# A fused spectral mixer and GEGLU block on one core: weight forms over five plain chunks, stores three steps later, transposes ahead of the down stage

## The chip, the cores and the metric

The kernel runs on one core of a Trainium2 chip. A core has a matrix engine (PE, with its weight loads PEld beside it), a vector engine (DVE), a scalar or activation engine (ACT), a general engine (POOL) and a queue engine (SP) that issues all of this kernel's DMA transfers. Each engine works through its own instructions in the order of the program and waits on semaphores for the others. The metric is the device time of one execution, the median over several runs.

## The reference

Two blocks act one after the other on 8192 tokens of 448 channels: a spectral block (Fourier transform over the tokens, a small complex two-layer network on each frequency in four channel blocks, soft threshold, inverse transform), and a gated feed-forward block of width 1792. Both are modulated by six rows that come from a condition vector.

```python
x = A_x
mod = (_silu(c) @ w_mod).reshape(c.shape[0], 6, 1, -1)
sa, ca, ga, sb, cb, gb = (mod[:, 0], ..., mod[:, 5])
h = _layernorm(x, axis=-1) * (1 + ca) + sa
x = x + ga * _A_ref(h, A_w1, A_b1, A_w2, A_b2)       # rfft, complex MLP, shrink, irfft
h = _layernorm(x, axis=-1) * (1 + cb) + sb
x = x + gb * _B_ref(h, B_w_gate, B_w_up, B_w_down)   # (gelu(h @ w_gate) * (h @ w_up)) @ w_down
```

## The kernel before

Up to 384.7 us the kernel makes the spectral part: it leaves the half-inverted spectrum in DRAM (`vd`). All that the change touches comes after that.

The second part goes over the tokens in 32 chunks of 256 (`CB` = 2 blocks of 128). For a chunk it loads `v` (spectrum), `g` (a slice of the inverse transform) and `xx` (the input), finishes the inverse transform on PE, adds the residual into a tile `x1`, normalizes to `n`, packs `n` as a high and a low half in float16 into `pk`, and turns `pk` into `nt` by transposing DMA transfers. Then PE forms gate and up products for 1792 columns, ACT and DVE make the activation `x`, it is quantized into two halves `ac`, and the down stage multiplies by `wd` and adds the result to `x1`, which goes to `out`.

There are two ways to form gate and up:

- **Plain chunks**, the first `NSTD` = 4. A chunk has 14 steps k (`gate_up(i, k)`), each 20 products of 128x256. At step k = 2 stands the down stage of the chunk before (`down(i - 1)`), with three places inside it (`mid(0)`, `mid(1)`, `mid(2)`, called m0, m1 and m2 below) where other work may be put.
- **Winograd chunks**, all later ones. They use the Strassen-Winograd scheme: sums and differences of weight parts and of token parts, in 7 products in place of 8. A chunk has 7 periods (`period(u)`), one for each pair of weight tiles, and the down stage of the chunk before stands at period `LA` = 2, in `phase(i)`.

The Winograd scheme needs the weights in another form. In the plain chunks 1 to 3 the kernel makes these forms for 7 weight tiles: `load_forms` loads a tile into `wr`; `form_sums` forms sums on POOL; `forms_hi` writes the high halves into `ws` on ACT (L1557); `forms_lo` writes the low halves on DVE (L1561); `store_forms` sends `ws` to DRAM (`wk`). Each tile has two parts that are stored apart, made of four pieces (0 and 1, 2 and 3). All tiles use one `wr`, and both parts use one `ws`. A table `prep` says after which step each of these calls stands: a tile takes six steps.

In the Winograd chunks PE reads the forms from four slots (`wslot`), which `load_part` refills from `wk` (L1269). `load_part` also fills the slots for the first time, at steps 4, 7, 11 and 13 of the last plain chunk.

Nothing but the order of the program sets which work comes first on an engine: the schedule is written out by hand, in the tables `prep`, `hooks`, `second` and `first` for plain chunks and `extra` for Winograd chunks. In `extra`, a key is the period within the chunk, and each entry names how many chunks ahead it works. The packing (`wpack_hi` on ACT, L1321, and `wpack_lo` on POOL) is held back to the next period. `wtransposes` (L1333) issues the transposes of `pk`, one at period 1 and four at period 2. `phase(i)` comes ahead of the entries of `extra` at period 2, and the store of the output (L1241) is the last thing that `down` issues. The pools `cq`, `cp2` and `wp` hold one buffer for each tag unless a number is given.

The names in the profile: `pgu` and `set` are the PSUM banks of plain and Winograd products, `pdn` those of the down stage, `pi` those of the inverse, `sb` a copy of part of `set` that ACT makes (L1378) and DVE adds back (L1387).

Of the kernel before, what the change touches and what calls it, by code (L numbers as in the profile page):

```python
# [39 lines left out]
LA = 2  # L40
NSTD = 4
WPARTS = ((0, 4), (4, 7))
# [7 lines left out]
def spectral_geglu(ctx, tc, x, w1, b1, w2, b2, wg, wu, wd, cvec, wmod, cf1, cs2, cmi, cgm, out):  # L50
# [924 lines left out]
    with ExitStack() as cctx:  # L975
# [4 lines left out]
        pkt = cp.tile([128, NXT * 128], F16, name="pk")  # L980
        nts, acts, pgu = {}, {}, {}

# [213 lines left out]
        def down(i, banks, mid=lambda n: None):  # L1196
# [43 lines left out]
            if not last:  # L1240
                dma(ov[:, i * CB : (i + 1) * CB, :], x1)  # L1241

# [224 lines left out]
        def phase(i):  # L1467
# [66 lines left out]
        def form_cuts(t, part):  # L1534

            w, r, s2 = raws[("s", t)], raws[("w", t)], raws[("f", t)].rearrange("p (c x) -> p c x", c=3)
            tq = r[:, :, 6:7]
# [25 lines left out]
        def store_forms(t, part):  # L1563
            w = raws.pop(("s", t))
            if part == 0:
                G.tensor_copy(w[:, :, 3, 0:3], w[:, :, 2, 0:3])
            for pr, rows in enumerate(rows2):
                for r, c in zip(rows2, range(2)):
                    dma(wk[t][part][r, pr], w[rows, :, c::2])

        prep = {}
        for n in range(NP):
            for s, fn, *args in (
                (0, load_forms),
                (1, form_sums, 0),
                (1, forms_hi, 0),
                (2, forms_lo, 0),
                (2, forms_hi, 1),
                (2, forms_lo, 1),
                (3, form_sums, 1),  # L1580
                (3, store_forms, 0),
                (4, forms_hi, 2),
                (4, forms_hi, 3),
                (4, forms_lo, 2),
                (5, forms_lo, 3),
                (5, store_forms, 1),
            ):
                prep.setdefault(NFT + 6 * n + s, []).append((fn, n, *args))
        for s, k in enumerate((4, 7, 11, 13)):
            for part in range(2):  # L1590
                prep.setdefault((NSTD - 1) * NFT + k, []).append((lambda u, part: load_part(u, part), U0 + s, part))

# [72 lines left out]
        V.tensor_scalar(gb_r, gb_r, ds_d, None, op0=ALU.mult)  # L1665

        def two_banks(q):
            return bank("pc" if q == 1 else "pd", "pdn")

        def steps0(n):  # L1670
            for fn, *args in second[("down", None, "down2")[n]] if n != 1 else []:
                fn(2, *args)

        for i in range(NSTD):
# [4 lines left out]
            for k in range(NFT):  # L1679
# [5 lines left out]
                if i == 1:  # L1685
                    for fn, *args in second.get(k, []):
                        fn(2, *args)
                if k == 2 and i > 0:
# [21 lines left out]

        load_v(NSTD + 2)
        load_g(NSTD + 2)
        for u in range(U0, NT_ + 1):
            period(u)
            i, k = divmod(u, NP)
            if i == nch:
                continue
            flush()
            if k == LA:
                phase(i)  # L1720
            for d, fn, *args in extra[k]:
                if i + d < nch:
                    if fn in (wpack_hi, wpack_lo):
                        held.append((fn, i + d, *args))
                    else:
                        fn(i + d, *args)
        late = {
            0: lambda: [on(NT_ - 1, joins), on(NT_ - 1, gel3), on(NT_ - 3, quant_lo), on(NT_ - 1, mult3), on(NT_ - 1, stage_d), on(NT_ - 1, gel1), on(NT_ - 1, mult1), on(NT_ - 2, quant_hi), sums(xs[NT_ - 1], V)],
# [79 lines left out]
```

## Time and profile before

| | us |
|---|---|
| Median of 3 runs (lowest to highest) | 2153.84 (2153.24 to 2154.56) |
| Profiled execution, its own time | 2148.29 |
| Span of its instructions | 2146.5 |
| Busy: PE | 1919.0 (89%) |
| Busy: DVE, POOL, ACT | 1467.5, 1177.7, 1022.5 |

A row of a wait list names the waiting engine and line, the one it waited for, the total, the number of times and the longest. A row of a line group names line, engine, operation, out<-in and count, then busy time and the mean of one in ns, then the engine's idle time just before these instructions and what ended most of it. A row of the timeline gives start, length, engine, line and operation, and in brackets the idle time before and its releaser; SPq is the queue of DMA issues. The granted PE clock is a share of full speed, averaged over a stretch.

### The profile page before, as it was taken

The numbers are of one execution on the slowest core, as the hardware profiler recorded it, in microseconds if no ns is written. First come the engines' busy times: TensorE is split into PE (matmuls) and PEld (weight loads), VectorE is DVE, ScalarE is ACT, GpSimd is POOL, SyncE is SP. The second block draws the span as 40 slices with busy tenths as digits, with TensorE's granted clock in tenths as the row PEclk, the third lists the DMA queues.
The fourth block names the chain that finished last, engine by engine and source line by source line (L and its number), as shares of the span: only waits on it lengthen the run. The fifth ranks groups of instructions, "written<-read, shape, count | busy, mean of one in ns | idle before, by whom it ended". The sixth has DMA issues, their size and how long they took to land.

```text
span 2146.5 us, 58651 instructions
## 1 busy us (share of the span) xinstructions
PE 1919.0 (89%) x24284; PEld 1817.2 (85%) x24284; DVE 1467.5 (68%) x2957; ACT 1022.5 (48%) x1915; POOL 1177.7 (55%) x1643
## 2 busy tenths in 40 slices
PE   7899999886673899999999999999989999999998
PEld 3699998775552899999999999999989999999998
DVE  8677887755534576767676677777667676777744
ACT  5687887533322344444444444444444444444443
POOL 3166643455553565656565555666556565655633
PEclk9999999997876899999999999999999999999999
DMA  9998776544455755556565555555555555555562
GB/s 349 317 276 238 179 195 170 154 107 101 97 129 138 213 148 148 153 155 167 149 174 151 163 149 148 148 148 157 153 154 157 164 167 153 148 148 149 147 164 67
DMA packets 410308, 353.83 MB, mean 165 GB/s; under 512 B 115892, under 2 KB 388408, under 8 KB 410040
## 3 DMA queue, kind: packets, MB, share of 16 engines
q1 hardware_dynamic: 410040, 350.08, 57.9%
q8 instruction: 190, 3.11, 0.6%
q14 instruction: 78, 0.64, 0.1%
HBM read 265.34 MB, written 60.10 MB: 152 GB/s over the span
## 4 chain that ended last, share of the span: by engine, by line
PE 52%; DVE 14%; DMA 11%; POOL 9%; SPq 5%; ACT 4%; issue 4%; ACTq 0%; POOLq 0%; DVEq 0%
PE set L1350 25%; PE pdn L1193 4%; DMA nt<-pk 4%; PE pdn L1191 4%; PE pdn L1192 4%; DVE ac L1425 3%; POOL x L1206 3%; POOL o L1205 3%; PE set L1191 2%; PE set L1192 2%; PE set L1193 2%; SPq L1333 2%; DVE ws L1561 1%; DVE y L471 1%; PE ps L210 1%
## 5 line engine op out<-in xcount | busy, mean ns | idle before, releaser
L1350 PE MATMUL set<-nt,wk 128*128 128x128 f16 x15288 | 911.1, 224 | 111.4 <-ACT sb L1378 76.8
L1350 PEld LDWEIGHTS <-wk 128*128 128x128 f16 x15288 | 901.1, 101 | 119.2 <-issue 117.1
L1191 PE MATMUL pdn<-wd,ac 128*128 128x224 f16 x1162 | 303.1, 261 | 12.3 <-ACT ac L1178 11.7
L1193 PE MATMUL pdn<-wd,ac 128*128 128x224 f16 x1162 | 302.7, 260 | 3.3 <-DVE ac L1179 2.1
L1192 PE MATMUL pdn<-wd,ac 128*128 128x224 f16 x1162 | 302.8, 261 | 0.0
L1425 DVE SCALAR_TENSOR_TENSOR ac<-x,sa_act,ac 128x896 f16<-128x896 f32 x196 | 277.0, 1414 | 1.3 <-ACT ac L1415 1.3
L1167 POOL TENSOR_TENSOR x<-x 128x128 f32<-128x128 f32 x223 | 120.3, 539 | 251.4 <-DVE x L1403 142.4
L1403 DVE TENSOR_TENSOR x<-c,gl 128x384 f32<-128x384 f32 x196 | 179.0, 913 | 109.8 <-ACT gl L1399 109.7
L1399 ACT ACTIVATE gl<-c,dg 128x384 f32<-128x384 f32 x196 | 120.5, 615 | 275.1 <-DVE c L1393 271.8
L1415 ACT ACTIVATE ac<-x,sa_act 128x896 f16<-128x896 f32 x196 | 202.3, 1032 | 0.6 <-DVE x L1170 0.4
L1118 PE MATMUL pgu<-nt,wk 128*128 128x256 f16 (+1 forms) x1232 | 154.5, 295 | 44.0 <-DVE x L1159 43.9
L1234 POOL TENSOR_TENSOR o<-u,p 128x224 f32<-128x224 f32 x32 | 21.0, 658 | 306.0 <-DVE u L1233 299.6
L1118 PEld LDWEIGHTS <-wk 128*128 128x128 f16 (+1 forms) x1232 | 121.8, 105 | 76.6 <-issue 54.7
L1387 DVE TENSOR_TENSOR c<-set,sb 128x512 f32<-128x512 f32 x196 | 134.6, 687 | 74.2 <-PE set L1350 74.2
L1191 PEld LDWEIGHTS <-ac 128*128 128x128 f16 x1568 | 154.0, 98 | 19.2 <-ACT ac L1178 12.2
L1193 PEld LDWEIGHTS <-ac 128*128 128x128 f16 x1568 | 154.1, 98 | 4.9 <-DVE ac L1179 2.8
L1192 PEld LDWEIGHTS <-ac 128*128 128x128 f16 x1568 | 154.2, 98 | 0.5
L1378 ACT COPY sb<-set 128x512 f32<-128x512 f32 x196 | 113.7, 580 | 73.1 <-PE set L1350 71.8
L1168 POOL TENSOR_TENSOR x<-x 128x128 f32<-128x128 f32 x223 | 126.6, 568 | 17.5
L471 DVE SCALAR_TENSOR_TENSOR y<-pm,t 64x224 f32<-64x224 f32 x256 | 99.5, 388 | 39.1 <-ACT t L463 35.1
L1327 POOL TENSOR_TENSOR pk<-tf,pk 128x128 f16<-128x128 f32 (+2 forms) x84 | 92.5, 1115 | 52.8 <-ACT pk L1321 52.8
L115 POOL TENSOR_TENSOR yl<-y,yh 128x448 fp32r<-128x448 f32 x63 | 76.6, 1216 | 73.7 <-ACT yh L113 57.9
(323 smaller groups left out, 3970.3 us busy)
## 6 DMA issues: line engine op xcount, KB each, us to landing
wk<-wk SPq DMA_DIRECT2D x88, 1024.0 KB, 7.3
wk<-wk SPq DMA_DIRECT2D x88, 768.0 KB, 5.4
tr<-td SPq DMA_DIRECT2D x64, 224.0 KB, 4.9
vd<-us SPq DMA_DIRECT2D x64, 224.0 KB, 3.1
xx<-in_A_x SPq DMA_DIRECT2D x32, 448.0 KB
v<-vd SPq DMA_DIRECT2D x63, 224.0 KB, 5.5
out<-x SPq DMA_DIRECT2D x31, 448.0 KB
xt<-in_A_x SPq DMA_DIRECT2D x15, 896.0 KB, 16.2
```

What stands on the lines that cost most here:

```text
L471: V.scalar_tensor_tensor(y[ri * 64 : ri * 64 + 64, gi], pv[si, ri], LAM, tv[si, ri], op0=ALU.add, op1=ALU.min)
L1118: T.matmul(pgu[i, t, q][:, pr * H : (pr + 1) * H], ws[rows, n, w, tw], nts[i][rows, tn, :], start=start, stop=stop, skip_group_check=True,)
L1168: e.tensor_tensor(s2, s1, a11, ALU.subtract)
L1191: T.matmul(ps, ac[:, 0, ka], w[:, 0, kb], start=n == 0, stop=False)
L1192: T.matmul(ps, ac[:, 0, ka], w[:, 1, kb], start=False, stop=False)
L1193: T.matmul(ps, ac[:, 1, ka], w[:, 0, kb], start=False, stop=n == NP - 1)
L1350: T.matmul(ps2[:, pr, reg * 128 : reg * 128 + 128], slot[:, pr, hl, wt, :], nt[:, xt, :], start=start and j == 0, stop=j == len(terms) - 1 ...
L1387: V.tensor_tensor(c[:, :, 1:3, :], p[:, :, 0:256].rearrange("p g (r c) -> p g r c", r=2), b[:, :, 0:128].rearrange("p g (o c) -> p g o c", ...
L1399: S.activation(gls[u], cts[u][:, 0], AF.Gelu_apprx_tanh, scale=dg)
L1403: V.tensor_tensor(xs[u][:, 1::3, :], cts.pop(u)[:, 1], gls.pop(u), ALU.mult)
L1415: S.activation(ac[:, 0], xs[u][:, 0:7], AF.Copy, scale=sa_act[:, t : t + 1])
L1425: V.scalar_tensor_tensor(ac[:, 1], xs.pop(u)[:, 0:7], sa_act[:, t : t + 1], ac[:, 0], op0=ALU.mult, op1=ALU.subtract)
```

## The change

`NSTD` becomes 6, so 6 chunks are plain and 26 take the Winograd way. The forms are made in chunks 1 to 5. Their calls are placed by a time in us within the plain stage (33 us from tile to tile), which `plan` turns into a step or one of the places m0 to m2 of the down stage by a list of 48.2 us for a chunk. Part 0 and part 1 each have a `ws` of their own. Calls of `prep` now stand ahead of the down stage at step 2. The output's store is taken out of `down`: `store_out` issues it after the down stage of step 5 in plain chunks and after period 4 in Winograd chunks (`down` stands at 2 in both). In `extra` the split of `v` moves to period 0, the loads of `v` and `g` for the next chunks change places, and `phase` comes after the entries of period 2. The token sums of chunks 6 and 7 use the buffer `o` of the down stage. `v` and `g` of chunk 8 are loaded at step 9 of the last plain chunk; before, those of chunk 6 were loaded after it.

```diff
-NSTD = 4
+NSTD = 6
@@ down
             if not last:
-                dma(ov[:, i * CB : (i + 1) * CB, :], x1)
+                outs.append((i, x1))
@@ token_sums
-                nxt[i]["t"] = cq.tile([128, 2 * D], F32, tag="tf", name="tf")
+                nxt[i]["t"] = cq.tile([128, 2 * D], F32, tag="o", name="tf") if i < NSTD + 2 else cp2.tile([128, 2 * D], F32, tag="tf", name="tf")
@@ extra
-            0: [],
-            1: [(2, split_v), (2, split_g), (1, wtransposes, [0])],
+            0: [(2, split_v)],
+            1: [(2, split_g), (1, wtransposes, [0])],
...
-            5: [(2, wpack_hi, [3]), (2, wpack_lo, [3]), (3, load_g)],
-            6: [(2, wpack_hi, [4]), (2, wpack_lo, [4]), (3, load_v)],
+            5: [(2, wpack_hi, [3]), (2, wpack_lo, [3]), (3, load_v)],
+            6: [(2, wpack_hi, [4]), (2, wpack_lo, [4]), (3, load_g)],
@@ forms_hi
-                raws[("s", t)] = cp2.tile([128, 2, 4, 4 - part // 2, 128], F16, tag="ws", name="ws")
+                raws[("s", t, part // 2)] = cp2.tile([128, 2, 4, 4 - part // 2, 128], F16, tag=f"ws{part}", name="ws")
@@ the table of the forms
+        spots = [(0, 2.4), (1, 4.9), (2, 7.3), ("m0", 11.3), ("m1", 13.3), ("m2", 17.4)]
+        spots += [(k, 21.4 + 2.44 * (k - 2)) for k in range(3, NFT)]
         prep = {}
+        def plan(us, fn, *args):
+            i, r = divmod(us, 48.2)
+            i, p = next(((1 + int(i), p) for p, at in spots if at >= r), (2 + int(i), 0))
+            prep.setdefault((i, p), []).append((fn, *args))
         for n in range(NP):
-            for s, fn, *args in (
+            for us, fn, *args in (
                 (0, load_forms),
-                (1, form_sums, 0),
-                (1, forms_hi, 0),
...
-                (5, store_forms, 1),
+                (11, form_sums, 0),
+                (11, forms_hi, 0),
...
+                (28, store_forms, 1),
             ):
-                prep.setdefault(NFT + 6 * n + s, []).append((fn, n, *args))
+                plan(33 * n + us, fn, n, *args)
@@ the plain chunks
+                for fn, *args in prep.pop((i, k), []):
+                    fn(*args)
                 if k == 2 and i > 0:
-                    down(i - 1, two_banks, steps0 if i == 1 else lambda n: None)
+                    down(i - 1, two_banks, lambda n: steps_std(i, n))
...
+                if k == 5:
+                    store_out()
+                if (i, k) == (NSTD - 1, 9):
+                    load_v(NSTD + 2)
+                    load_g(NSTD + 2)
-                for fn, *args in first.pop(i * NFT + k, []) + prep.pop(i * NFT + k, []):
+                for fn, *args in first.pop(i * NFT + k, []):
@@ the Winograd chunks
             if i == nch:
                 continue
+            if k == LA + 2:
+                store_out()
             flush()
-            if k == LA:
-                phase(i)
             for d, fn, *args in extra[k]:
...
+            if k == LA:
+                phase(i)
```

Two places show what this does to the order of the engines. The first is SP's queue in an early Winograd chunk, chunk 5 of before and chunk 7 of the change: `wk<-wk` is a refill of a slot, `nt<-pk` the transposes, `out<-x` the store, and `v`, `g` and `xx` the loads. Before:

```order
L1333 DMA_TRANSPOSE nt<-pk 128x5x128
L1269 DMA wk_3379<-wk_65 128x8x384
L1269 DMA wk_3377<-wk_60 128x8x512
L1241 DMA out<-x_5746 128x896
L1333 DMA_TRANSPOSE nt<-pk 128x5x128 x4
L1269 DMA wk_3378<-wk_63 128x8x384
L1269 DMA wk_3377<-wk_61 128x8x384
L909 DMA g<-cgm 128x256
L911 DMA xx<-in_A_x 128x896
L917 DMA v<-vd 128x2x224 x2
```

With the change:

```order
L1333 DMA_TRANSPOSE nt<-pk 128x5x128
L1269 DMA wk_3379<-wk_65 128x8x384
L1269 DMA wk_3377<-wk_60 128x8x512
L1333 DMA_TRANSPOSE nt<-pk 128x5x128 x4
L1269 DMA wk_3378<-wk_63 128x8x384
L1677 DMA out<-x_3369 128x896
L1269 DMA wk_3377<-wk_61 128x8x384
L917 DMA v<-vd 128x2x224 x2
L909 DMA g<-cgm 128x256
L911 DMA xx<-in_A_x 128x896
```

The four transposes have moved ahead of the store, the store stands behind one more refill, and `v` comes ahead of `g`.

The second place is ACT in plain chunk 1, from the end of the first weight tile's forms (`ws<-wr`) to the start of the second's; `gel` is the activation of a gate and up step and `ac` the quantization. Before:

```order
L1557 ACTIVATE ws<-wr,sww 128x256
L1154 ACTIVATE gel<-pgu,dg 128x256
L1178 ACTIVATE ac<-x_6737,sa_act 128x896
L1154 ACTIVATE gel<-pgu,dg 128x256 x2
L1178 ACTIVATE ac<-x_6785,sa_act 128x896
L1557 ACTIVATE ws<-wr,sww 128x3x128
L1557 ACTIVATE ws<-wr,sww 128x128
```

With the change:

```order
L1557 ACTIVATE ws<-wr,sww 128x256
L113 CAST gh<-g 128x256
L113 CAST vh<-v 128x896
L1154 ACTIVATE gel<-pgu,dg 128x256 x2
L1178 ACTIVATE ac<-x_6738,sa_act 128x896
L1154 ACTIVATE gel<-pgu,dg 128x256 x2
L1178 ACTIVATE ac<-x_6795,sa_act 128x896
L1154 ACTIVATE gel<-pgu,dg 128x256 x2
L1178 ACTIVATE ac<-x_6894,sa_act 128x896
L1154 ACTIVATE gel<-pgu,dg 128x256 x2
L1178 ACTIVATE ac<-x_6937,sa_act 128x896
L1154 ACTIVATE gel<-pgu,dg 128x256
```

Between two tiles' forms stood three activations, and now there are nine; the next row of the change is the second tile's first form.

More of the change, by code (lines that the diff above doesn't have):

```diff
@@ L980, in spectral_geglu @@
         pkt = cp.tile([128, NXT * 128], F16, name="pk")
-        nts, acts, pgu = {}, {}, {}
+        nts, acts, pgu, outs = {}, {}, {}, []
         def nt_tile():
@@ L1534, in form_cuts @@
         def form_cuts(t, part):
-            w, r, s2 = raws[("s", t)], raws[("w", t)], raws[("f", t)].rearrange("p (c x) -> p c x", c=3)
+            w, r, s2 = raws[("s", t, part // 2)], raws[("w", t)], raws[("f", t)].rearrange("p (c x) -> p c x", c=3)
             tq = r[:, :, 6:7]
@@ L1563, in store_forms @@
         def store_forms(t, part):
-            w = raws.pop(("s", t))
+            w = raws.pop(("s", t, part))
             if part == 0:
@@ L1569, in store_forms @@
                     dma(wk[t][part][r, pr], w[rows, :, c::2])
+        spots = [(0, 2.4), (1, 4.9), (2, 7.3), ("m0", 11.3), ("m1", 13.3), ("m2", 17.4)]
+        spots += [(k, 21.4 + 2.44 * (k - 2)) for k in range(3, NFT)]
         prep = {}
+        def plan(us, fn, *args):
+            i, r = divmod(us, 48.2)
+            i, p = next(((1 + int(i), p) for p, at in spots if at >= r), (2 + int(i), 0))
+            prep.setdefault((i, p), []).append((fn, *args))
         for n in range(NP):
-            for s, fn, *args in (
+            for us, fn, *args in (
                 (0, load_forms),
-                (1, form_sums, 0),
-                (1, forms_hi, 0),
[L1577 to L1585, printed above, removed]
-                (5, store_forms, 1),
-            ):
-                prep.setdefault(NFT + 6 * n + s, []).append((fn, n, *args))
-        for s, k in enumerate((4, 7, 11, 13)):
+                (11, form_sums, 0),
+                (11, forms_hi, 0),
+                (11, forms_lo, 0),
+                (14, forms_hi, 1),
+                (14, forms_lo, 1),
+                (17, form_sums, 1),
+                (19, store_forms, 0),
+                (20, forms_hi, 2),
+                (20, forms_lo, 2),
+                (23, forms_hi, 3),
+                (23, forms_lo, 3),
+                (28, store_forms, 1),
+            ):
+                plan(33 * n + us, fn, n, *args)
+        for n, k in enumerate((4, 7, 11, 13)):
             for part in range(2):
-                prep.setdefault((NSTD - 1) * NFT + k, []).append((lambda u, part: load_part(u, part), U0 + s, part))
+                prep.setdefault((NSTD - 1, k), []).append((lambda u, part: load_part(u, part), U0 + n, part))
         hooks = {
@@ L1665, in spectral_geglu, with store_out, steps_std @@
         V.tensor_scalar(gb_r, gb_r, ds_d, None, op0=ALU.mult)
+        def store_out():
+            for i, x1 in outs:
+                dma(ov[:, i * CB : (i + 1) * CB, :], x1)
+            outs.clear()
         def two_banks(q):
             return bank("pc" if q == 1 else "pd", "pdn")
-        def steps0(n):
-            for fn, *args in second[("down", None, "down2")[n]] if n != 1 else []:
+        def steps_std(i, n):
+            for fn, *args in second[("down", None, "down2")[n]] if i == 1 and n != 1 else []:
                 fn(2, *args)
+            for fn, *args in prep.pop((i, f"m{n}"), []):
+                fn(*args)
         for i in range(NSTD):
@@ L1726, in spectral_geglu @@
                         fn(i + d, *args)
+            if k == LA:
+                phase(i)
+        store_out()
         late = {
```

3 lines of the change are left out of this document (1 added, 2 removed).

## Prediction

> **What bounds the kernel now.** I read the table of stretches first, cut where the down stage's first vector instruction (L1219) starts, then the lists of waits in the two stages that the change touches, then the instruction rows behind the largest waits. The columns of the stretches: time, busy time of PE, its weight load, DVE, ACT and POOL, granted PE clock, DMA share, GB/s.
>
> ```profile
> L1219 DVE TENSOR_TENSOR o<-pdn,p x32: 379/392/392, 438.6 to 2132.9; 128x224 f32<-128x224 f32 x32
> 384.70:438.60 53.90, 51.03 (x446) 42.29 (x444) 43.74 (x84) 28.50 (x42) 27.61 (x37) 0.97 0.56 153
> 438.60:523.20 84.60, 56.67 (x450) 45.65 (x449) 45.87 (x81) 26.94 (x50) 45.51 (x53) 0.83 0.39 96
> 523.20:607.00 83.80, 57.22 (x460) 46.88 (x459) 43.96 (x79) 27.71 (x54) 47.62 (x60) 0.83 0.45 106
> 607.00:719.20 112.20, 65.49 (x591) 56.10 (x590) 42.27 (x80) 29.05 (x57) 50.00 (x60) 0.74 0.62 165
> 719.20:1998.60 1279.40, 1198.46 (x17477) 1180.26 (x17476) 907.11 (x1725) 570.60 (x1100) 764.87 (x1125) 0.97 0.55 156
> 1998.60:2094.00 95.40, 91.37 (x1389) 90.96 (x1388) 56.03 (x109) 42.47 (x79) 42.71 (x74) 0.98 0.51 140
> 2094.00:2146.50 52.50, 44.77 (x611) 43.62 (x608) 26.77 (x51) 17.61 (x31) 18.44 (x30) 1.00 0.19 61
> ```
>
> The reader is to see two stages. From 438.6 to 607.0 each plain chunk takes 84 us with PE busy for 57 and no other engine for more than 48: nothing is full, so waits set the pace. The third stretch, 112.2 us, holds the rest of the last plain chunk and the switch to the Winograd chunks. From 719.2 on, 25 Winograd chunks take 1279.4 us, 51.2 each, with PE busy 94%.
>
> The waits of the three slow stretches, and PE's idle time in them by line:
>
> ```profile
> DVE ws L1561 <- ACT ws L1557: 73.7, 9, 10.8
> ACT ws L1557 <- DMA wk<-ws: 72.8, 7, 14.6
> ACT ws L1557 <- DMA wr<-in_B_w_up: 51.1, 6, 14.4
> L1118 PE MATMUL pgu<-nt,wk 128*128 128x256 f16 (+1 forms) x860 | 111.9, 302 | 41.1 <-DVE x L1159 41.1
> L1193 PE MATMUL pdn<-wd,ac 128*128 128x224 f16 x142 | 38.5, 271 | 2.1 <-DVE ac L1179 2.1
> L1191 PE MATMUL pdn<-wd,ac 128*128 128x224 f16 x141 | 38.4, 272 | 11.7 <-ACT ac L1178 11.7
> L1350 PE MATMUL set<-nt,wk 128*128 128x128 f16 x186 | 14.4, 254 | 34.1 <-DVE x L1159 29.0 <-ACT sb L1378 4.4 <-ACT set L1382 0.6
> L1020 PE MATMUL pi<-v,gh 128*128 128x448 f32 x6 | 3.5, 578 | 3.9 <-POOL v L115 3.9
> L1018 PE MATMUL pi<-vh,gh 128*128 128x448 f32 x6 | 3.2, 526 | 4.7 <-ACT vh L113 4.7
> L1019 PE MATMUL pi<-vh,gl 128*128 128x448 f32 x6 | 3.1, 516 | 3.5 <-POOL gl L115 3.5
> ```
>
> ACT stands still for 72.8 us because the one buffer `ws` of the weight forms is still being stored, and for 51.1 because a weight tile has not landed. DVE's half of the forms waits behind ACT (73.7), the activation's product L1159 stands behind that in DVE's queue, and PE waits for it (41.1 and 29.0).
>
> In the Winograd stage the rows are these: over the whole stage, then one chunk, engine by engine.
>
> ```profile
> ACT pk L1321 <- DMA nt<-pk: 120.1, 26, 5.7
> PE set L1350 <- ACT sb L1378: 72.4, 26, 3.9
> 1194.97 1.33 POOL L1206 TENSOR_TENSOR x<-o,x 128x448 f32<-128x448 f32 x1
> 1196.33 0.37 SPq L1241 DMA_DIRECT2D out<-x  x1
> 1196.76 6.02 SPq L1333 DMA_TRANSPOSE nt<-pk  x4
> 1201.60 0.41 ACT L1321 CAST pk<-n 128x256 f16<-128x256 f32 x1 [4.67 <-DMA nt<-pk]
> 1202.42 0.56 ACT L1378 COPY sb<-set 128x512 f32<-128x512 f32 x1
> 1203.04 0.66 PE L1350 MATMUL set<-nt,wk 128*128 128x128 f16 x9 [2.83 <-ACT sb L1378]
> ```
>
> The output store waits in SP's queue for POOL's last addition. The four transposes stand behind the store, ACT cannot write `pk` until they have read it, and PE waits 2.83 us for the copy that ACT makes next. It happens once in each of 26 chunks: 72.4 / 26 = 2.8 us each.
>
> **The change, part by part.** The prices of a plain chunk on PE come from these rows, and those of a Winograd chunk from two stretches with one chunk each:
>
> ```profile
> 393.87 7.04 PE L1118 MATMUL pgu<-nt,wk 128*128 128x256 f16 x63
> 432.78 0.26 PE L1191 MATMUL pdn<-wd,ac 128*128 128x224 f16 x1
> 446.77 0.26 PE L1193 MATMUL pdn<-wd,ac 128*128 128x224 f16 x1
> 462.09 0.57 PE L1018 MATMUL pi<-vh,gh 128*128 128x448 f32 x1
> 462.83 0.57 PE L1020 MATMUL pi<-v,gh 128*128 128x448 f32 x1
> 1333.30:1383.90 50.60, 48.12 (x703) 47.42 (x701) 36.33 (x70) 22.91 (x45) 30.59 (x45) 0.97 0.53 152
> 1742.10:1791.40 49.30, 46.54 (x701) 45.72 (x699) 36.24 (x69) 22.63 (x44) 30.59 (x45) 1.00 0.58 170
> L1350 PE MATMUL set<-nt,wk 128*128 128x128 f16 x546 | 31.2, 219 | 2.4 <-ACT sb L1378 2.1 <-DVE c L1393 0.2
> 2018.97 1.26 PE L1350 MATMUL set<-nt,wk 128*128 128x128 f16 x18 [2.07 <-ACT sb L1378]
> ```
>
> *Two chunks more are plain.* The gate and up products start every 0.109 us (7.04 less the last one's 0.27, over 62 steps); 1232 of them for 4 chunks on the page make 308 a chunk, 33.6 us. The 147 down products run from 432.78 to 447.03, 14.25 us. The inverse is 6 products 0.37 apart, 2.2. PE alone needs 50.1 us. To this I add the inverse's own waits for its split inputs, 3.9 + 4.7 + 3.5 over three chunks, 4.0 each, which come from POOL's and ACT's work right behind the down stage and which nothing here removes; and 1.0 for the clock, as in the first stretch (0.97 of 53.9 us). A plain chunk then takes 55.1, with 50.1 as its lower end.
>
> *The forms are spread, with a buffer for each part.* Seven tiles in five chunks are 1.4 a chunk, against 2.3 before. ACT no longer waits for a store (72.8 us go), since the second part has its own `ws`. The load now stands 11 us ahead of its first use in the plan's numbers, where it stood one step ahead, so the 51.1 go too as long as SP is free. What PE lost through these, 41.1 + 29.0 + 11.7 + 2.1, I take as gone; if a tile's whole load wait of 8.5 us (51.1 / 6) were left on PE, 1.4 tiles would add 12 us to a chunk. No engine becomes the bound: DVE's 45.9 and POOL's 47.6 busy us a chunk hold more tiles than a chunk will have, and both lie under 55.
>
> *The switch.* The last forms stand at step 7 of chunk 5, 15 us before its end by the plan. The stretch then holds 11 of 14 gate and up steps (26.4), a down stage (14.25), two inverses (4.4, the second bounded by the first), 186 Winograd products at 31.2 / 546 = 0.057 (10.6), the inverse's waits (4.0), the first copies' 4.4 + 0.6, and 1.0 for the clock: 65.7, where 112.2 stood. The transfers for chunk 6 (five transposes, then a tile's load) now meet in SP's queue at chunk 5's start; I leave 10 us for that in the range.
>
> *Transposes ahead of the down stage, store at step 4.* The four transposes are issued when PE begins the inverse and the 14.25 us of down, some 20 us before ACT wants `pk`; they took about 6 us. ACT's wait goes, and PE's with it: 49.3 - 2.1 = 47.2 us for a chunk at full clock. The lower end is PE's busy 46.5. The store's wait for POOL stays, but behind it stand only a refill and the loads of `v`, `g` and `xx`. What is late next is POOL's and DVE's forming of the chunk, with 30.6 and 36.2 busy us of 47: no bound. Splitting `v` one step earlier and loading it one step earlier cancel. The shared buffer of `o` and the token sums touches chunks 6 and 7 only, and I put it at nothing: 11 us of steps lie between the packing and the down stage's first write. If that cover failed, POOL's packing would hold DVE once or twice for a few us.
>
> *The sum*, against the profiled span of 2146.5: 438.6 to the first down stage, unchanged; 4 plain chunks at 55.1, 220.4; the switch 65.7; 23 Winograd chunks at 47.2, 1085.6; the two chunks without packing 95.4 less the wait of 2.1 and 1.5 of clock, 91.8; the end 52.5. That is 1954.6, 191.9 less. The profiled execution's own time is 2148.3 and the median of the runs 2153.8, so the runs should show about 1962. Seen by stage: 438.6 to the Winograd chunks took 280.6 and will take 286, with two more chunks in it; the rest is two chunks of 51 saved and 25 made 4 us shorter.
>
> [...] My 47.2 takes it that the clock stays full once the wait is gone. The two one-chunk rows above both have a wait of 2.1 us, the one a clock of 0.97, the other 1.00; between 100 and 380 us, where PE hardly waits, the clock held:
>
> ```profile
> 100.00:380.00 280.00, 268.82 (x2497) 258.65 (x2496) 225.08 (x481) 218.85 (x375) 155.03 (x164) 0.99 0.79 215
> ```
>
> I read this as the waits pulling the clock down, not each time. [...]
>
> **The rivals.** *The clock drops stay.* The mean chunk of 51.2 less its wait of 2.8 is 48.4, 1.2 above 47.2; 23 times that is 28 us: 1990. For it speaks the 0.97 beside a wait of 2.1, against it the stretch at 0.99. 12%.
>
> *The forms still hold the plain chunks*, now through SP's one queue, in which a tile's load stands behind stores and transposes. With the full 12 us a chunk in five chunks the time is 2022, with half of it 1992. 12%.
>
> *The Winograd wait does not go*, because ACT or PE meets another wait at the same place (the refills `wk`, which follow in the same queue). 23 chunks at 51.2 add 92: 2054. 4%.
>
> *Slower than before.* Plain chunks cannot do it alone: with everything else as summed, 478 us would have to go into four chunks and the switch, 93 a chunk, above the 84 of now. It takes a loss in each of 25 Winograd chunks of more than (2158 - 1962) / 25 = 7.8 us. The one candidate is `v`, now loaded behind the delayed store and split at step 0:
>
> ```profile
> v<-vd SPq DMA_DIRECT2D x63, 224.0 KB, 5.5
> 1153.33 1.06 SPq L917 DMA_DIRECT2D v<-vd  x2
> 1170.95 0.93 ACT L113 CAST vh<-v 128x896 fp32r<-128x896 f32 x1
> ```
>
> Issued at 1153.3, landed 5.5 us later, used at 1171: 11 us spare. It decides only if `v` comes some 20 us later than now. 3%.
>
> **The numbers.** The forecast keeps 69%, with 1932 (plain chunks, switch and Winograd chunks near their lower ends) to 1985 as its own range. I stretch the range to 2010, which takes in the first rival and the lower half of the second and leaves out some 17%. A change within 0.2% is what a measurement here cannot tell from none; faster by more 96%, the same 1%, slower 3%.
>
> **What would show it.** Right: no wait of ACT for `ws` stores or of DVE behind it, plain chunks at 52 to 58 us between L1219's starts, the 29 us hole ahead of the first Winograd product gone, `pk` no longer waiting for `nt`, Winograd chunks at 47 with a clock of 1.00. Wrong: half-clock rows in a stage without gaps (first rival), ACT waiting for `wr` (second), PE waiting for `wk` or `sb` once a chunk (third), ACT's split waiting for `v` (fourth).

## The result, and the profile after

The changed kernel takes 1955.57 us (median of 4 runs, 1953.62 to 1957.64) where the kernel before took 2153.54 beside it: a ratio of 0.9085, 95% interval 0.9067 to 0.9103. The forecast was 1962 with a range of 1932 to 2010. The profiled execution took 1953.62 us, its span is 1951.8.

The stretches of the changed kernel, cut like those of before at the starts of the down stage's first vector instruction (time, busy time of PE, weight load, DVE, ACT and POOL, granted PE clock, DMA share, GB/s):

```profile
L1219 DVE TENSOR_TENSOR o<-pdn,p x32: 375/392/393, 439.9 to 1938.8; 128x224 f32<-128x224 f32 x32
  POOL pk L1327: 1.0, 1
439.90:499.50 59.60, 53.48 (x478) 45.80 (x476) 43.26 (x75) 25.06 (x46) 42.71 (x49) 0.94 0.37 91
499.50:549.60 50.10, 47.51 (x433) 41.48 (x431) 32.80 (x62) 19.64 (x35) 39.85 (x49) 0.97 0.52 133
549.60:609.80 60.20, 52.81 (x467) 44.91 (x466) 38.05 (x66) 23.13 (x43) 38.98 (x45) 0.91 0.40 94
609.80:666.40 56.60, 50.67 (x462) 44.10 (x461) 37.77 (x69) 23.06 (x44) 42.87 (x53) 0.97 0.47 117
666.40:748.00 81.60, 60.23 (x589) 52.52 (x588) 40.20 (x69) 24.80 (x47) 46.55 (x58) 0.85 0.69 188
748.00:1810.50 1062.50, 1061.60 (x16079) 1050.20 (x16077) 831.53 (x1587) 526.78 (x1012) 793.32 (x1035) 1.00 0.64 172
1810.50:1899.90 89.40, 89.36 (x1390) 89.24 (x1388) 55.84 (x109) 42.52 (x80) 45.31 (x74) 1.00 0.56 150
1899.90:1951.80 51.90, 44.80 (x611) 43.65 (x608) 26.79 (x51) 17.60 (x31) 18.44 (x30) 0.99 0.20 63
```

The reader is to see three things. In the 23 Winograd chunks PE is busy for 1061.6 of 1062.5 us at full clock: 46.2 us a chunk, where 51.2 stood. The four plain chunks take 56.6 us on average, where 84 stood. The switch between the two takes 81.6, and that is the one stretch in which PE still loses much.

Set against the terms of the sum:

| us | forecast | measured | difference |
|---|---|---|---|
| to the first down stage | 438.6 | 439.9 | +1.3 |
| 4 plain chunks | 220.4 | 226.5 | +6.1 |
| the switch | 65.7 | 81.6 | +15.9 |
| 23 Winograd chunks | 1085.6 | 1062.5 | -23.1 |
| 2 chunks without packing | 91.8 | 89.4 | -2.4 |
| the end | 52.5 | 51.9 | -0.6 |
| sum | 1954.6 | 1951.8 | -2.8 |

That the total came so near is luck: two errors cancel, the switch (15.9 us too short in the forecast) and the Winograd chunks (23.1 us too long).

**The Winograd chunk.** PE's groups over the stretch of 25 chunks before, then over the 23 of the change:

```profile
L1350 PE MATMUL set<-nt,wk 128*128 128x128 f16 x13650 | 812.7, 224 | 72.7 <-ACT sb L1378 70.3 <-DVE c L1393 1.5
L1460 PE MATMUL set<-vh,gh 128*128 128x448 f32 x50 | 20.9, 419 | 8.2 <-DVE x L1410 8.2
```

```profile
L1350 PE MATMUL set<-nt,wk 128*128 128x128 f16 x12558 | 711.6, 219 | 0.9
```

Before, PE idled 72.7 + 8.2 us, 3.2 a chunk; that is gone. The rest of the 5.0 us is PE's busy time: it was 1198.46 / 25 = 47.9 a chunk and is 1061.60 / 23 = 46.2. Most of that is clock: before, 77.9 us of PE's busy time lay in pieces at half clock; an estimate of what they cost is half of it, 39 us, or 1.6 a chunk. SP's queue in one chunk of the change, and ACT's write to `pk` in it, show why the wait went (start, length):

```profile
1200.72 2.21 SPq L1333 DMA_TRANSPOSE nt<-pk  x1
...
1205.21 9.22 SPq L1333 DMA_TRANSPOSE nt<-pk  x4
...
1224.42 0.37 SPq L1677 DMA_DIRECT2D out<-x  x1
1224.66 0.66 ACT L1321 CAST pk<-n 128x192 f16<-128x192 f32 x2
```

The four transposes are issued by 1214.4 (1205.21 + 9.22), ten us ahead of ACT's next write to `pk`, and the store stands behind them. No wait of ACT for `nt<-pk` is left in this stretch.

**Plain chunks and switch.** PE's idle time in the four plain chunks, 439.9 to 666.4, and then the largest waits in the switch, 666.4 to 748:

```profile
L1118 PE MATMUL pgu<-nt,wk 128*128 128x256 f16 (+1 forms) x1232 | 141.2, 281 | 8.7 <-DVE x L1159 8.7
L1193 PE MATMUL pdn<-wd,ac 128*128 128x224 f16 x193 | 50.0, 259 | 1.8 <-DVE ac L1179 1.8
L1191 PE MATMUL pdn<-wd,ac 128*128 128x224 f16 x192 | 49.7, 259 | 1.7 <-DVE u L1227 0.7 <-ACT p L1224 0.7 <-ACT ac L1178 0.3
L1020 PE MATMUL pi<-v,gh 128*128 128x448 f32 x8 | 4.3, 538 | 4.1 <-POOL v L115 4.1
L1018 PE MATMUL pi<-vh,gh 128*128 128x448 f32 x8 | 4.0, 498 | 4.0 <-ACT vh L113 4.0
L1019 PE MATMUL pi<-vh,gl 128*128 128x448 f32 x8 | 3.8, 478 | 1.8 <-POOL gl L115 1.8
```

```profile
POOL wr L1528 <- DMA wr<-in_B_w_up: 10.2, 1, 10.2
ACT ws L1557 <- DMA wr<-in_B_w_up: 9.4, 1, 9.4
PE pi L1019 <- POOL gl L115: 8.2, 1, 8.2
...
DVE x L1029 <- DMA out<-x: 7.2, 1, 7.2
PE pgu L1118 <- DVE x L1159: 4.9, 2, 2.6
```

In the plain chunks 22 us of PE's waits are left in all, 5.5 a chunk, and no engine waits for the stores of `ws`. One weight tile comes late there too: its load, issued at 549.91 behind four transposes of 5.16 us, keeps POOL waiting 8.0 us and ACT 4.7. In the switch the last weight tile comes late (10.2 on POOL, 9.4 on ACT), and DVE waits 7.2 us in one piece for an output store. SP's queue and that instruction of DVE show where both come from:

```profile
663.84 7.78 SPq L1333 DMA_TRANSPOSE nt<-pk  x5
671.66 1.33 SPq L1519 DMA_DIRECT2D wr<-in_B_w_gate  x2
...
702.67 2.37 SPq L1677 DMA_DIRECT2D out<-x  x1
712.91 1.16 DVE L1029 TENSOR_TENSOR x<-pi,ga_r 128x448 f32<-128x448 f32 x2 [7.22 <-DMA out<-x]
```

The load of the seventh tile stands behind five transposes that take 7.8 us to issue. The store, issued at 702.67, is still reading the tile `x1` whose buffer the residual of a later chunk (L1029) is about to overwrite; DVE, and all that stands behind it on DVE, waits until 712.9.

### The profile page after: what moved, and what is told of

The parts are those of the page before. It is cut to its first block, busy times and chain, and to the rows that moved or that the text cites. A ratio compares the mean times of both kernels' runs of the same rounds, so it can differ in the third digit from the quotient of the medians.

```text
span 1951.8 us, 57569 instructions
## 1 busy us (share of the span) xinstructions
PE 1867.3 (96%) x23808; PEld 1767.8 (91%) x23808; DVE 1451.8 (74%) x2919; ACT 1010.4 (52%) x1879; POOL 1276.7 (65%) x1633
## 4 chain that ended last, share of the span: by engine, by line
PE 71%; DVE 10%; POOL 6%; DMA 5%; issue 3%; ACT 2%; SPq 2%; ACTq 0%; POOLq 0%; DVEq 0%
PE set L1350 40%; PE pdn L1193 5%; PE pdn L1191 5%; PE pdn L1192 5%; PE ps L210 2%; PE set L1193 2%; PE set L1191 2%; PE set L1192 2%; DVE y L471 1%; PE pgu L1118 1%; DMA wr<-in_B_w_up 1%; DVE ws L1561 1%; POOL x L1167 1%; DMA raw<-in_B_w_up 1%; SPq L1569 1%
## 5 line engine op out<-in xcount | busy, mean ns | idle before, releaser
L1350 PE MATMUL set<-nt,wk 128*128 128x128 f16 x14196 | 805.9, 219 | 7.5 <-ACT sb L1378 3.5
L1350 PEld LDWEIGHTS <-wk 128*128 128x128 f16 x14196 | 798.4, 98 | 12.9 <-issue 10.7
L1193 PE MATMUL pdn<-wd,ac 128*128 128x224 f16 x1190 | 308.3, 259 | 3.0 <-DVE ac L1179 1.8
L1191 PE MATMUL pdn<-wd,ac 128*128 128x224 f16 x1190 | 308.5, 259 | 2.3 <-DVE u L1227 0.7
L1192 PE MATMUL pdn<-wd,ac 128*128 128x224 f16 x1190 | 308.2, 259 | 0.0
L1399 ACT ACTIVATE gl<-c,dg 128x384 f32<-128x384 f32 x182 | 112.2, 616 | 275.5 <-DVE c L1393 274.4
L1425 DVE SCALAR_TENSOR_TENSOR ac<-x,sa_act,ac 128x896 f16<-128x896 f32 x182 | 229.6, 1261 | 16.1 <-ACT ac L1415 16.0
L1118 PE MATMUL pgu<-nt,wk 128*128 128x256 f16 (+1 forms) x1848 | 214.1, 282 | 16.2 <-DVE x L1159 16.2
L1118 PEld LDWEIGHTS <-wk 128*128 128x128 f16 (+1 forms) x1848 | 175.3, 101 | 54.7 <-issue 30.3
L1403 DVE TENSOR_TENSOR x<-c,gl 128x384 f32<-128x384 f32 x182 | 191.5, 1052 | 18.5 <-ACT gl L1399 18.5
L1167 POOL TENSOR_TENSOR x<-x 128x128 f32<-128x128 f32 x223 | 126.9, 569 | 118.7 <-DVE x L1159 50.2
L1415 ACT ACTIVATE ac<-x,sa_act 128x896 f16<-128x896 f32 x182 | 188.2, 1034 | 3.4 <-DVE x L1170 0.4
L1170 POOL TENSOR_TENSOR x<-x 128x128 f32<-128x128 f32 x223 | 175.5, 787 | 0.0
L1387 DVE TENSOR_TENSOR c<-set,sb 128x512 f32<-128x512 f32 x182 | 124.5, 684 | 43.6 <-PE set L1350 43.6
L1169 POOL TENSOR_TENSOR x<-x 128x128 f32<-128x128 f32 x223 | 147.5, 661 | 0.0
```

The costliest lines, as they stand in the source:

```text
L1118: T.matmul(pgu[i, t, q][:, pr * H : (pr + 1) * H], ws[rows, n, w, tw], nts[i][rows, tn, :], start=start, stop=stop, skip_group_check=True,)
L1167: e.tensor_tensor(s1, a21, a22, ALU.add)
L1169: e.tensor_tensor(s3, a11, a21, ALU.subtract)
L1170: e.tensor_tensor(s4, a12, s2, ALU.subtract)
L1191: T.matmul(ps, ac[:, 0, ka], w[:, 0, kb], start=n == 0, stop=False)
L1192: T.matmul(ps, ac[:, 0, ka], w[:, 1, kb], start=False, stop=False)
```

## The experiments

The theory was that the gain has two independent parts. The order of the transposes in the Winograd chunks takes away a wait and, with it, drops of the clock. The forms take away waits in the plain chunks, by the two buffers and by the spread over more chunks. Against it stood these: the store's later place (two periods in the Winograd chunks, three steps in the plain ones) carries the Winograd gain; one of the two edits to the forms does nothing; the clock has nothing to do with PE's wait. Two more questions came from the traces: what made the switch long, and whether the late store is of any use.

**1. The Winograd part alone, on the kernel before.** Four plain chunks with the old table of forms and one `ws`; `v`'s split and load, `phase` and the store as in the change.

```diff
-            0: [],
-            1: [(2, split_v), (2, split_g), (1, wtransposes, [0])],
+            0: [(2, split_v)],
+            1: [(2, split_g), (1, wtransposes, [0])],
...
+            if k == LA + 2:
+                store_out()
             flush()
-            if k == LA:
-                phase(i)
             for d, fn, *args in extra[k]:
...
+            if k == LA:
+                phase(i)
```

> Of the change, only the Winograd chunks' part: transposes ahead of the down stage, store after period 4, split and loads of v and g as in the change. The plain chunks stay at four, with the forms and stores as before. Theory (the two parts act apart): the four plain chunks and the switch keep their 280 us, and each full Winograd chunk falls from 51.2 to the 46.2 us of the changed kernel with a clock of 1.00, 25 x 5.0 = 125 us, and about 6 us in the last two: a span near 2016 us. Rival (the parts need each other, since the stores and loads of the first stage set how the second starts): chunks stay above 48 us, a span above 2065.

Measured: 2025.14 us, ratio 0.9422 (0.9386 to 0.9458), span 2024.3. The stretches, the last two plain chunks with the switch and then 25 Winograd chunks:

```profile
440.30:727.10 286.80, 179.82 (x1491) 149.70 (x1490) 130.26 (x239) 83.79 (x161) 141.93 (x171) 0.78 0.49 126
727.10:1881.80 1154.70, 1153.76 (x17478) 1141.58 (x17476) 903.42 (x1725) 572.57 (x1101) 862.44 (x1125) 1.00 0.63 172
```

The Winograd chunk takes 46.2 us, as in the full change, while the stretch ahead of it, 286.8 us, is no faster than before (280.6). Those 6 us more, which are not explained here, are most of what the span lies above the 2016 that was expected. The gain of the Winograd stage owes nothing to the forms.

**2. The forms alone.** The change, with the Winograd chunks put back to their old order.

```diff
-            0: [(2, split_v)],
-            1: [(2, split_g), (1, wtransposes, [0])],
+            0: [],
+            1: [(2, split_v), (2, split_g), (1, wtransposes, [0])],
...
-            if k == LA + 2:
-                store_out()
             flush()
+            if k == LA:
+                phase(i)
+                store_out()
             for d, fn, *args in extra[k]:
...
-            if k == LA:
-                phase(i)
```

> The changed kernel with the Winograd part undone: phase ahead of the transposes again, the store right behind it, split and loads of v and g in their old places; six plain chunks with spread forms stay. Theory: Winograd chunks return to 51.2 us, 23 x 5.0 = 115 us and some 6 us in the last two, a span near 2072 us. PE waits again for the copy to sb once a chunk, 2.8 us. Rival: with the plain stage changed the wait is another one, and the chunks come out below 49 us, a span below 2020.

Measured: 2068.26 us, ratio 0.9623 (0.9575 to 0.967), span 2063.5. Four plain chunks, and 23 Winograd chunks:

```profile
438.80:661.80 223.00, 200.79 (x1812) 173.50 (x1810) 151.54 (x271) 90.45 (x165) 163.73 (x194) 0.95 0.44 108
742.20:1914.00 1171.80, 1100.21 (x16079) 1083.66 (x16078) 835.29 (x1588) 525.03 (x1012) 703.52 (x1035) 0.97 0.55 156
```

The plain chunks have the whole of their gain (55.8 each), the Winograd chunks next to none of theirs (50.9 each). With the order of before, its waits are back in these 23 chunks: ACT's for `nt<-pk`, 104.0 us, and PE's for `sb`, 61.8 us, 2.7 a chunk. By span the first part alone gives 122 us, the second alone 83, both 195. The sum, 205, is 10 too many because in the change two chunks fewer get the 5 us.

**3. The store at once, in the Winograd chunks.** The change, with the store issued right after the down stage and the transposes still ahead of it.

```diff
-            if k == LA + 2:
-                store_out()
...
             if k == LA:
                 phase(i)
-        store_out()
+                store_out()
```

> The changed kernel, but in Winograd chunks the output's store stands right behind the down stage, so behind the transposes and ahead of the refill of period 3; all else as in the change. Theory A (the order of transposes and down stage is the whole gain): chunks at 46.2 to 46.5 us, a span of 1952 to 1960. Theory B (the store's later place is needed too): the refill behind the store is issued only when POOL's last addition ends, some 6 us after the down stage, and lands after PE wants it, so PE waits 1 to 5 us for wk in every chunk: 1975 to 2070.

Measured: 1951.34 us, ratio 0.9079 (0.9045 to 0.9112), span 1950.0. The Winograd stretch and SP's wait in it:

```profile
745.80:1808.70 1062.90, 1061.92 (x16080) 1050.27 (x16078) 832.38 (x1588) 527.18 (x1012) 793.75 (x1035) 1.00 0.63 172
SPq L1677 <- POOL x L1206: 232.3, 23, 11.0
```

SP now stands still for 10 us in each chunk, and it costs nothing: 46.2 us as with the late store. What carries the gain of this stage is then the order of transposes and down stage, with the earlier split of `v` and the swapped loads, which no run takes apart. The traces speak for the transposes: the wait of ACT for `nt<-pk` (116.2 us in 25 chunks) is what went, and ACT waits for `v` neither before nor after.

**4. One `ws` for both parts.** The change, with the one buffer of before.

```diff
-... tag=f"ws{part}", name="ws")
+... tag="ws", name="ws")
```

> The changed kernel with one buffer ws for both parts of a weight tile, as before; the spread over five chunks and all the order stay. Theory (the buffers count on their own): ACT waits for each tile's first store before it can make the second part, 7 waits of 4 to 14 us, and a plain chunk rises from 56.7 us by 5 to 15: a span of 1975 to 2025. Rival (the spread is enough, since SP and ACT now have time between the parts): less than 8 us more, a span below 1960.

Measured: 1998.89 us, ratio 0.93 (0.9253 to 0.9347), span 2000.1. Four plain chunks, and ACT's wait up to the first Winograd chunk:

```profile
441.60:717.90 276.30, 211.56 (x1833) 180.21 (x1831) 140.60 (x270) 90.34 (x166) 159.90 (x194) 0.86 0.36 88
ACT ws L1557 <- DMA wk<-ws: 86.0, 7, 18.0
```

The wait for the store comes back once for each of seven tiles, and a plain chunk takes 69.1 us. The span is 48 us longer, and the four plain chunks are 50 longer (276.3 against 226.5): all of it is there. The spread alone does not hide the store.

**5. Two buffers without the spread.** Experiment 1 with a `ws` for each part (and the token sums in the buffer `o`, as in the change).

```diff
-... tag="ws", name="ws")
+... tag=f"ws{part}", name="ws")
```

> The Winograd part of the change on four plain chunks, with the forms placed as before, but with a buffer ws for each part (and the shared buffer of o, to make room). It asks whether the spread over five chunks is needed once the buffers are there. Theory (both count: seven tiles in three chunks leave ACT waiting for the tile loads, 51 us of waits for wr before, and for POOL): the stretch from the first down stage to the first Winograd one falls from 287 us to 230 to 260, a span of 1967 to 1997, still behind the changed kernel's 1952. Rival (the buffer alone does it): below 222 us, a span under 1959, so that four plain chunks are as good as six.

Measured: 1989.68 us, ratio 0.9259 (0.9227 to 0.9291), span 1989.7. Up to the first Winograd chunk:

```profile
439.50:693.30 253.80, 172.47 (x1488) 146.28 (x1486) 137.78 (x240) 83.93 (x160) 146.32 (x171) 0.84 0.56 143
ACT ws L1559 <- DMA wr<-in_B_w_up: 46.2, 6, 13.6
```

Against experiment 1 the buffers give 35 us of span (2024.3 to 1989.7). Left over is the wait for the weight tile, 46.2 us in six pieces, nearly the 51.1 of before, since the table still loads a tile one step ahead of its use. What then still separates this kernel from the change gives the other 38 (1989.7 to 1951.8): two more plain chunks and the new plan with its earlier loads, of tiles above all. These are not taken apart here. Neither the buffers nor the spread gives the whole gain alone.

**6 and 7. The clock by itself.** The change, with a few copies of no use on ACT in the middle of each Winograd chunk, ahead of the copy `sb` that PE waits for; eight in one kernel, six in the other. The copies write a tile that nobody reads.

```diff
+        def idle_copies(n):
+            junk = cp2.tile([128, 512], F32, tag="junk", name="junk")
+            for _ in range(n):
+                S.copy(junk[:, 0:D], gb_r)
...
+            if k == LA + 1 and i + 2 < nch:
+                held.append((idle_copies, 8))
```

> The changed kernel with eight idle copies (128x448, about 0.45 us each by ACT's rows of that size) on ACT ahead of the packing of period 4, once in each Winograd chunk: a wait for PE of about the size of the one removed (1.5 to 3 us), without any transfer in it. Theory (the wait itself pulls the clock down): half-clock stretches come back in about every second chunk, and a chunk takes 46.2 plus the wait plus up to 1.5 us. [...]

> As the kernel with eight copies, with six: the wait comes out about 0.9 us shorter. Theory: with the wait near 1 us the clock stays 1.00 in most chunks, so between this and eight copies a chunk grows by more than two copies' time. [...]

Measured, one run each: 2056.04 us with eight (span 2054.3) and 2007.59 with six (span 2005.8). The Winograd stretch and PE's group in it, eight and then six:

```profile
750.40:1908.70 1158.30, 1092.35 (x16079) 1077.62 (x16078) 845.05 (x1588) 623.93 (x1196) 734.17 (x1035) 0.97 0.58 158
L1350 PE MATMUL set<-nt,wk 128*128 128x128 f16 x12558 | 742.3, 223 | 66.0 <-ACT sb L1378 62.2 <-DVE c L1393 2.8
```

```profile
746.00:1862.00 1116.00, 1069.51 (x16078) 1051.88 (x16076) 844.17 (x1587) 593.97 (x1150) 734.82 (x1035) 1.00 0.60 163
L1350 PE MATMUL set<-nt,wk 128*128 128x128 f16 x12558 | 719.6, 219 | 46.5 <-ACT sb L1378 34.8 <-DVE c L1393 10.7
```

ACT is busy 97.2 and 67.2 us longer than in the change, 0.53 and 0.49 us for each copy, where 0.45 was expected. With eight copies PE waits 2.7 us for `sb` in each chunk, much as before the change, and a half-clock piece of 3.41 us comes back in 17 of 23 chunks. With six it waits 1.5 us, and the clock holds in all of them. PE's busy time with eight copies is 1092.35 - 1061.60 = 31 us above the change; 56.5 us of it lie in half-clock pieces, and half of that, 28, is an estimate of what the clock cost. With six it is 8 us above, at full clock, so something other than the clock adds to it; what, stays open. So waits of 2.7 us brought the clock down here, but not every time. Two waits of the kernel with eight copies show both cases; the stretches are cut at 1226.13, where a half-clock piece starts, and in steps of its 3.41 us from there:

```profile
1225.04 7.14 PE L1350 MATMUL set<-nt,wk 128*128 128x128 f16 x93 [2.69 <-ACT sb L1378]
1275.77 2.67 PE L1350 MATMUL set<-nt,wk 128*128 128x128 f16 x42 [2.70 <-ACT sb L1378]
1222.72:1226.13 3.41, 1.08 (x17) 0.96 (x17) 1.58 (x3) 3.38 (x9) 1.78 (x5) 1.00 1.02 319
1226.13:1229.54 3.41, 3.41 (x36) 3.41 (x34) 3.38 (x7) 1.75 (x5) 2.02 (x4) 0.50 0.60 221
1270.50:1273.92 3.42, 2.52 (x43) 2.28 (x41) 1.51 (x3) 3.23 (x7) 1.60 (x3) 1.00 0.64 224
1273.92:1277.33 3.41, 1.56 (x26) 1.44 (x26) 2.02 (x4) 3.41 (x9) 2.26 (x6) 1.00 1.03 325
```

Around the first wait PE is busy for 1.08 of 3.41 us, and the next stretch runs at 0.50. Around the second, equally long, the two stretches have 2.52 and 1.56 us busy, and both run at 1.00. The last section counts the half-clock pieces of more runs.

**8. The seventh tile's load earlier.** The change, with that one call 8 us earlier in the plan, which puts it ahead of the five transposes.

```diff
-                plan(33 * n + us, fn, n, *args)
+                plan(33 * n + us - 8 * (fn is load_forms and n == NP - 1), fn, n, *args)
```

> The changed kernel with the seventh tile's load eight us earlier in the plan, so that it stands ahead of the five transposes at the start of chunk 5 in SP's queue. Theory (the switch takes 81.6 us and not 65.7 because this load lands 10 us late and POOL's and ACT's queues back up behind it): the waits of 10.2 us of POOL and 9.4 us of ACT for wr go, PE's 8.2 and 2.2 us at the inverse shrink to 4 in all, and the switch takes 68 to 74 us: a span of 1938 to 1945. Rival (the late output store, whose landing DVE waits for, or POOL's own work sets it): 78 us or more, a span of 1948 or above.

Measured: 1946.38 us, ratio 0.906 (0.9043 to 0.9076), span 1945.1. The switch, and the wait that is left:

```profile
667.50:741.20 73.70, 59.70 (x589) 51.98 (x587) 37.45 (x70) 24.93 (x47) 46.19 (x58) 0.91 0.76 205
DVE x L1029 <- DMA out<-x: 7.8, 1, 7.8
```

The switch is 7.9 us shorter, and DVE's wait for the store stays.

**9. The last plain chunk's store earlier as well.** Experiment 8 with that store at step 3.

```diff
-                if k == 5:
+                if k == (5 if i < NSTD - 1 else 3):
```

> As the kernel with the earlier load, and the output store of chunk 5 after its step 3 in place of 5, ahead of the seventh tile's first store and the first slot's load. Theory: DVE's wait of 7.2 us for that store's landing, which holds PE for 2.6 and 2.4 us, goes too: 3 to 5 us below the kernel with the earlier load alone. Rival (once the load is early, SP is free and the store in time anyway): within 1 us of it.

Measured: 1935.61 us, ratio 0.9012 (0.8994 to 0.9031), span 1932.0. The switch:

```profile
663.70:728.20 64.50, 55.01 (x589) 49.88 (x588) 37.35 (x69) 24.92 (x47) 46.17 (x59) 0.97 0.84 222
```

Another 9.2 us off the switch, where 3 to 5 were expected. Of them 4.7 are PE's busy time (59.70 to 55.01), as the granted clock went from 0.91 to 0.97. The two causes together account for the switch: 64.5 us without them, where the forecast had 65.7.

**10. All plain stores at once.** The change, with every plain chunk's store right after its down stage, and nothing else.

```diff
-                if k == 5:
+                if k == 2:
```

> The changed kernel with the output store of plain chunks right behind the down stage (step 2) in place of step 5; all else as in the change. Theory A (the later store in plain chunks keeps SP free for the forms' stores and loads): SP stands some 6 us at the store in each of five chunks with form transfers behind it, and the span rises by 3 to 15 us. Theory B (the later store only makes its landing late for the residual that overwrites the tile, DVE's 7.2 us in the switch): the span falls by 3 to 6 us.

Measured: 1944.71 us, ratio 0.905 (0.9028 to 0.9073), span 1939.9.

```profile
661.80:736.40 74.60, 57.43 (x590) 51.27 (x589) 40.02 (x70) 24.81 (x47) 46.55 (x59) 0.91 0.75 202
SPq L1677 <- POOL x L1206: 42.9, 5, 16.1
```

The switch is 7 us shorter though the late tile is still there; DVE no longer waits for the store. SP stands still for 42.9 us at the five stores of the plain chunks, and these chunks take no longer for it (223.7 us against 226.5). The span is 11.9 us shorter, twice what was expected for this side: 7.0 at the switch, 2.8 in the plain chunks, and 1.8 ahead of them, where the two kernels do the same.

**11. Both.** Experiment 8 with all plain stores at once.

```diff
-                plan(33 * n + us, fn, n, *args)
+                plan(33 * n + us - 8 * (fn is load_forms and n == NP - 1), fn, n, *args)
...
-                if k == 5:
+                if k == 2:
```

> The kernel with the seventh tile's earlier load, and the stores of all plain chunks right behind the down stage in place of steps 5 and 3. By theory A of the store at once it is 3 to 15 us above the kernel with early load and store at step 3 of chunk 5 (span 1932); by theory B within 2 us of it, or below.

Measured: 1934.96 us, ratio 0.9005 (0.8981 to 0.9029), switch 64.4. It is the same as experiment 9 within the spread of the runs; both are about 1% below the change. The later store gained nothing in the Winograd chunks (experiment 3), and in the plain chunks it cost 7 to 9 us at the switch (experiments 9 to 11).

## Why the prediction was right, and where it was off

- **Waits set the pace, no engine is full: right.** In the plain chunks and the switch ACT's wait for the store of `ws` is gone, and its wait for the weight tile fell from 51.1 us in six pieces to 14.1 in two (4.7 and 9.4); in the Winograd chunks PE's wait for `sb` is gone. Each came back where its cause was put back (experiments 4, 5 and 2).
- **Transposes ahead of the down stage: the mechanism right, the term too long by 1.0 us a chunk (47.2 against 46.2).** In taking 49.3 - 2.1 the step removed one releaser of one line. That chunk's PE was idle for 49.3 - 46.54 = 2.8 us, part of it ahead of the inverse (L1460, 8.2 us over the stage), and all of it went. That makes 46.5, the step's own "lower end". The other 0.3 is PE's busy time at full clock, 46.2 against 46.54 in that chunk; the kernel with six copies, also at full clock and with waits, has 0.3 a chunk more than the change (46.5), so PE's busy time seems to shrink a little with its waits, and why is not shown. Over 23 chunks the term is 23 us too long, the largest error of the sum.
- **The clock: right.** The prediction took it that the wait pulls the clock down, not each time; the drops went with the wait (0.97 before, 1.00 with the change) and came back with one of about the same size (2.7 us and 0.97 in experiment 6). The first rival, in which they stay, fell.
- **Plain chunks: 55.1 against 56.6, on a sum with two wrong parts.** The forecast of 52 to 58 us holds for their mean, 56.6, and not one by one (59.6, 50.1, 60.2 and 56.6). PE's busy time is as forecast, 51.1 with the clock. Of waits 4.0 were forecast, all at the inverse; measured are 5.5, with 2.5 at the inverse, 2.2 for the activation L1159 and 0.9 in the down stage. "What PE lost through these I take as gone" was a little too much.
- **The switch: 65.7 against 81.6, the step that failed.** PE's busy time is 60.2, at a clock of 0.85, against 55.65 and 1.0 for the clock in the sum; the inverse's waits are 8.2 + 2.2 against 4.0; those of the gate and up products 4.9 against none; those of the first Winograd products 6.0 against 5.0. The tile's load behind five transposes was seen, and its 10 us left in the range instead of in the sum (7.9 measured). The other cause the prediction did not see: it costed the later store by what stands behind it in SP's queue, and never asked who overwrites the tile that the store reads. That is DVE's 7.2 us.
- **The second rival** (the forms hold the chunks through SP's queue) happened twice, each time with a tile's load behind transposes: once in the switch, and once in the third of the four plain chunks (POOL 8.0 us, ACT 4.7). There PE's longest wait, 4.0 us for ACT's `vh`, follows it, since ACT's cast of `v` stands behind a form that waited 6.4 us for POOL; no run loads that tile earlier. The third and fourth fell: in the 23 Winograd chunks PE waits for neither `sb` nor `wk`, and ACT not for `v`. In the fourth, the 93 us a chunk do not come out of its 478: with the switch as before they leave (478 - 112.2) / 4 = 91, with the forecast switch 103. Both lie above 84, so nothing turned on it.
- **The shared buffer `o`, put at nothing:** DVE's L1219 waited for POOL's packing once, 1.0 us.
- **The offset of 5.5 us** from the profiled execution to the median of the runs was 1.95 here (1953.62 to 1955.57). The forecast of 1962 lies 6.4 us above the median: 2.8 of them are the sum's, 3.6 this offset's.

## What to carry to other kernels

In a queue that issues in order, as SP's did here, put the transfer that somebody waits for ahead of the one that itself waits: the edit that did this, with an earlier split of `v` beside it, was worth 5 us in each of 25 chunks here, and delaying the one that waits was worth nothing. When a store is delayed, ask when its source is written again, as one asks of a load when it is read. When all of a PE wait's causes go, subtract PE's whole idle time in that stretch, and look at the clock beside it, since here waits of 2.7 us, once in each of 23 chunks, came with 31 us more of PE's busy time beside their own length (experiment 6).

## What the runs showed of the hardware

Pieces at half clock (a granted clock of 0.50) in these traces: in the Winograd chunks 19 before, none with the change, 19 with the forms alone, 17 with eight copies and none with six; in the plain chunks and the switch 11 before, 7 with the change, 12 with the Winograd part alone and 10 with one `ws`. Of the 19 before, 13 last 3.41 us and six 6.83; PE is busy for 0.48 to 0.73 of the first 3.41 us of these six, and what ends a piece is left open.

The length of a wait alone did not decide whether such a piece follows. In the kernel with eight copies one wait of 2.69 us has a piece behind it and one of 2.70 us has none (experiment 6). In the two chunks of the prediction it is the same: in the one with a clock of 0.97 PE's wait of 2.10 us ends at 1353.74 and a half-clock piece starts at 1354.38, in the one with 1.00 the wait of 2.13 us ends at 1762.49 and no piece follows. What does decide is not shown.

Five transposes of 128x5x128 took 7.8 us to issue on SP in the switch, and four 9.2 in a Winograd chunk where 6.0 stood before. No run tells what sets that.
